# Seven block products for eight in the second expert's first matrix product

## The chip, the core and the metric

One core of one Trainium2 chip runs the whole program in one launch. The metric is the device time in microseconds; 753.59 us is the median of three runs of the kernel before. TensorE (PE) multiplies, VectorE (DVE), ScalarE (ACT) and GpSimd (POOL) do the rest, SyncE (SP) issues nearly all DMAs.

## The reference

Inputs: q, k, v of 2 batches x 8 heads x 768 positions x 64; a projection of 64 x 6; two experts' weights `w_in` (512 x 2048) and `w_out` (2048 x 512). q, k, v and the projection are float32; the four weight matrices are float64.

```python
def _attn_ref(q, k, v, proj):
    q_bucket, k_bucket = ...            # six sign bits of q @ proj and k @ proj
    mask = q_bucket[:, :, :, None] == k_bucket[:, :, None, :]
    scores = np.where(mask, (1 / np.sqrt(D)) * np.matmul(q, k.transpose(0, 1, 3, 2)), -1e9)
    attn = softmax(scores)
    return np.matmul(attn, v)

def _moe_ref(x, w_in, w_out):           # first expert, 1536 tokens
    h = x @ w_in
    return (h * (1 / (1 + np.exp(-h)))) @ w_out

def _moe2_ref(x, w_in, w_out):          # second expert, on the first one's output
    h = x @ w_in
    return (h - np.tanh(h)) @ w_out
```

Attention's output, transposed to 1536 tokens x 512, goes through the first expert and its output through the second.

## The kernel before

Every product of the experts is done to nearly float32's precision out of pairs: an operand is kept as a high part (rounded to the matrix unit's fp32r format) and a low part (the rest), and each product of two 128-deep blocks is three matmuls, high x high, high x low, low x high, added up in one PSUM bank. Names end in `h` and `l` for the two parts (`xh`/`xl`, `gh`/`gl`, a weight set's `wh`/`wl`).

Tokens lie on the free axis in four blocks of 384 (`NB`); blocks 0 and 1 are batch 0, blocks 2 and 3 batch 1; two of them are a pair. The model dimension (512) is four tiles of 128 (`KD`), the hidden dimension (2048) four chunks (`NCH`) of four tiles of 128 (`F`). For each chunk and pair the loops of lines 876 to 963 run: first product (`h_mm`, L892: for each block and each `f` 4 x 3 = 12 matmuls of 128x128 by 128x384), then tanh (`h_tanh`, L896), the gate (`h_gate`, in place in PSUM, L902 for the first expert, L904 for the second), high part of g (`h_hi`, copied through the helper on L334), low part of g (`h_lo`, L910, PSUM minus high part), then the second product (`o_mm`, L954, also 12 matmuls for each block and output tile), whose bank is added to an accumulator in SBUF (`o_acc`, L961; the first chunk copies, L959).

`PASSES` (L696) sets three passes: first expert on pair 0 (while batch 1's attention still runs), first expert on pair 1, second expert on both pairs. After the first expert's last chunk its sums are halved and split into the second expert's `xh`/`xl` (L968, L971).

Weights arrive as 64-bit floats in pieces of 128 x 512 (`load_w`, L785); five steps make float32 of them: absolute value on ScalarE (L817), clip on GpSimd or VectorE (L820), shift, sign, low word on VectorE (L823, L827, L831); then the high part on ScalarE (L835) and the low part on GpSimd or VectorE (L839). In the first pass the float32 pieces are also stored to DRAM and fetched again in the second. Chunks 1 and 3 of the later passes have a second set of weight tiles (`ww2`).

The order of all instructions on all engines is worked out when the program is built: each piece of work is a task (`add`) with engines and costs, a due time (`key`), dependencies, and buffers that it takes; `Plan.order` (L92) repeatedly gives an engine the task that can start first, with ties within `slack` broken by due time. Constants of the plan stand in `KNOBS`. What results is a fixed order per engine; at run time each engine goes through its own list and waits on semaphores. After attention there are six PSUM banks for products (`banks`) and two for the conversion of weights (`cvs`).

Of the kernel before, what the change touches and what calls it, by code (L numbers as in the profile page):

```python
# [21 lines left out]
W_MIN = 2.0 ** -15  # L22
W_MAX = 2.0 ** 16 * (1.875 - 2.0 ** -23)

KNOBS = dict(start=1.134, step=2.53, gap=9.343, step1=3.92, ffn=3.61, ffn3=2.222, pv=12.257, prep=16.11, hash=8.464,
             slack=0.042, conv=33.419, conv0=52.708, vld=10.124, vmax=13.049, vsplit=16.427, x2=0.271, direct=0.4,
             direct1=0.083, b_qh=1.32, b_qlo=100, b_kup=100, b_vlo=2, b_bi=2.75, b_thi=100, b_shi=0.98, b_slo=100,
             b_xh=1.72, b_xlo=1.56, b_wlo=100, b_clip=-0.24, b_hhi=0.67, k_m=-0.273, k_e=0.107, k_t=1.899,
             k_th=2.064, k_tl=2.019, k_hi=1.332, k_lo=1.98, k_f=3.209, cj=3.559, cl=7.897, ahead=2, by=3.547,
             xsets=0, raws=5, vmax1=70.287, emode=1, lmode=1)  # L30


class Slot:
# [166 lines left out]
def lsh_attention_moe_kernel(  # L200
# [12 lines left out]
    nc = tc.nc  # L213
# [96 lines left out]
    wr_slots = [Slot(), Slot()]  # L310
    for i, s in enumerate(wr_slots):
        s.tag = f"w{i}"
    wt_slots = slots(wt, "wa", 2, [128, 512], I32, "wa")
    th_slots = slots(gt, "th", 2, [128, NB], F32, "th")

    def get(h):
# [386 lines left out]

    def switch_two():
        es.close()
        for i in range(3):
            late[f"ps_n{i}"] = ctx.enter_context(tc.tile_pool(name=f"ps_n{i}", bufs=1, space=PSUM))
        for i in range(2):
            late[f"ps_d{i}"] = ctx.enter_context(tc.tile_pool(name=f"ps_d{i}", bufs=1, space=PSUM))
        late["ww2"] = ctx.enter_context(tc.tile_pool(name="ww2", bufs=1))  # L710
        late["acc2"] = ctx.enter_context(tc.tile_pool(name="acc2p", bufs=1))
        xp2 = ctx.enter_context(tc.tile_pool(name="xp2", bufs=1))
        for blk in (2, 3):
            xh.append(xp2.tile([128, KD, NB], F32R, name=f"xh{blk}"))
            xl.append(xp2.tile([128, KD, NB], F32R, name=f"xl{blk}"))

    second = add("", 0.0, switch_two, 0, last_attn + [first], takes=shut2)
    for x in shut2:
        x.users += 1
    second.opens = (*m_late, *cv_late)  # L720

    xready = {0: list(xdone[0]), 1: list(xdone[1])}
    t_two = t_ffn + 128 * K["ffn"]
    for blk in (2, 3):
        xready[blk] = []
        for dt in range(KD):
            def x_hi2(blk=blk, dt=dt):
                nc.scalar.copy(xh[blk][:, dt, :], x32[:, dt, (blk % 2) * NB:(blk % 2 + 1) * NB])

            def x_lo2(e, blk=blk, dt=dt):  # L730
                src = x32[:, dt, (blk % 2) * NB:(blk % 2 + 1) * NB]
                ENG[e].tensor_tensor(xl[blk][:, dt, :], src, xh[blk][:, dt, :].bitcast(F32), op=ALU.subtract)
            y = add("ACT", 0.52, x_hi2, t_two + K["x2"] + 0.1 * dt + blk, [second])
            xready[blk] += [y, add(("POOL", "DVE"), (1.02, 0.57), x_lo2, t_two + K["x2"] + 0.1 * dt + blk, [y], port=("DVE",), give="xlo")]

    seq = [0]
    wslots = [(wtile["h0"], wtile["l0"]), (wtile["h1"], wtile["l1"])]
    w2slots = [(Slot(),), (Slot(),)]
    acc2_slots = [Slot(), Slot()]
    stored = {}  # L740
    pieces = [0]

    def t_group(k):
        return t_ffn + K["ffn"] * k if k < 128 else t_two + K["ffn3"] * (k - 128)

    for ps_i, (e, fresh, blks) in enumerate(PASSES):
        pairs = [blks[i:i + 2] for i in range(0, len(blks), 2)]
        accs = {}
        xnext = {}
        for c in range(NCH):  # L750
            base = seq[0]
            two = ps_i > 0 and c % 2 == 1
            wset = []
            for m in range(2):
                held = Held(w2slots[m] if two else wslots[m])

                def w_tiles(m=m, held=held, two=two):
                    if held.tile is None:
                        shape = [128, KD, FW] if m == 0 else [128, F, DM]
                        pool = late["ww2"] if two else ww  # L760
                        held.tile = tuple(pool.tile(shape, F32R, tag=f"{x}{m}", name="w" + x) for x in ("h", "l"))
# [4 lines left out]
                for j in range(4):  # L766
# [20 lines left out]
                    ld = add("SP", 0.35, load_w, kj - K["cl"], [second] * two + ([stored[ps_i - 1, c, m, j]] if not fresh else []),  # L787
                             takes=[w], tail=1.65 if fresh else 0.82)
                    prior = [first_take] if first_take else [ld]
                    if not fresh:  # L790
# [74 lines left out]
            for pi, pair in enumerate(pairs):  # L865
# [62 lines left out]
                for q, blk in enumerate(pair):  # L928
# [4 lines left out]
                    for d in range(KD):  # L933
                        tk = t_group(seq[0])
                        seq[0] += 1
                        bk = Held(*banks)
                        fresh_acc = c == 0 and pr not in accs
                        if fresh_acc:
                            accs[pr] = Held((acc_slot,) if e == 0 else (acc2_slots[pr],))
                        ah = accs[pr]  # L940

                        def acc_tile(ah=ah, e=e, pr=pr, d=d, half=half):
                            if ah.tile is None:
                                pool = accp if e == 0 else late["acc2"]
                                ah.tile = pool.tile([128, KD, S], F32, tag="acc" if e == 0 else f"acc{pr}", name="acc")
# [18 lines left out]
                        ac = add("DVE", 0.55, o_acc, tk + 1, [om] + ([second] if e else []),  # L964
                                 takes=[ah] if fresh_acc else [], uses=[bk] + ([] if fresh_acc else [ah]))
                        if c == NCH - 1 and e == 0:
                            def y_hi(blk=blk, d=d, acc_tile=acc_tile):
                                nc.scalar.activation(out=xh[blk][:, d, :], in_=acc_tile(), func=ACTF.Copy, scale=0.5)  # L968

                            def y_lo(e, blk=blk, d=d, acc_tile=acc_tile):  # L970
                                ENG[e].scalar_tensor_tensor(xl[blk][:, d, :], acc_tile(), 0.5,  # L971
                                                               xh[blk][:, d, :].bitcast(F32), op0=ALU.mult, op1=ALU.subtract)
                            x = add("ACT", 0.525, y_hi, tk + 1.5, [ac], uses=[ah])
                            y = add("DVE", 0.56, lambda y_lo=y_lo: y_lo("DVE"), tk + 2, [x], uses=[ah], port=True)
                            xnext.setdefault(blk, []).extend([x, y])
                        elif c == NCH - 1:
                            add("SP", 0.35, lambda blk=blk, d=d, f=acc_tile: nc.sync.dma_start(
                                out=outT[d * 128:(d + 1) * 128, blk * NB:(blk + 1) * NB], in_=f()), tk + 2, [ac],
                                uses=[ah], tail=0.6)
        xready.update(xnext)  # L980

    for t in plan.order(K["slack"]):
        plan.run(t)
# [53 lines left out]
```

## Time and profile before

| | us |
|---|---|
| runs: lowest, median, highest of 3 | 753.16, 753.59, 754.58 |
| profiled execution | 754.19 |
| its span, first to last instruction | 752.3 |
| TensorE busy | 718.0 |
| VectorE, ScalarE, GpSimd busy | 531.6, 430.0, 370.3 |

The span is one execution of the program as the hardware profiler saw it. An engine's busy time is the union of its instructions; for TensorE the ends of overlapping matmuls are modelled. A time that ended an engine's idle stretch is put down to the engine that released it.

### The profile page before, as it was taken

To read this page: it belongs to the slowest core of one execution; us is meant where nothing else is said; L and a number is where in the kernel's file an instruction comes from. 1 tells how busy PE (TensorE), PEld (TensorE's weight loads), DVE (VectorE), ACT (ScalarE), POOL (GpSimd) and SP (SyncE) were. 2 spreads that over 40 slices of the span, in tenths; PEclk is the share of its full clock that TensorE was granted. 3 is DMA by queue.
4 is the path that set the end of the run, shared out by engine and by line. 5 is a ranking of instruction groups with operands and counts; after the bars stand their busy time and mean duration, and the time that the engine had idled before them with its cause. 6 is when DMAs were issued, how large, how long until landed. Compare 5 with 4: busy or idle time off the path is not lost.

```text
span 752.3 us, 14254 instructions
## 1 busy us (share of the span) xinstructions
PE 718.0 (95%) x5486; PEld 694.4 (92%) x5486; DVE 531.6 (71%) x1002; ACT 430.0 (57%) x813; POOL 370.3 (49%) x247
## 2 busy tenths in 40 slices
PE   5679889899999999999999999999999999999998
PEld 4478777799999999999999999999999999999998
DVE  6789899998897898977433689884685576344342
ACT  5879999996895966866442526542451434122130
POOL 5658779678798865677453353540341152000000
PEclk9799999999999999999999999999999999999999
DMA  9698999979899995982333333330131030000102
GB/s 358 138 219 164 182 194 240 246 151 257 240 236 244 215 228 152 236 183 71 103 102 96 104 121 112 113 112 30 56 113 56 1 103 10 1 1 1 63 22 85
DMA packets 140446, 100.78 MB, mean 134 GB/s; under 512 B 117438, under 2 KB 119742, under 8 KB 140378
## 3 DMA queue, kind: packets, MB, share of 16 engines
q1 hardware_dynamic: 140090, 99.59, 53.3%
q8 instruction: 43, 0.70, 0.4%
q10 hardware_dynamic: 288, 0.28, 0.2%
q14 instruction: 25, 0.20, 0.1%
HBM read 57.95 MB, written 11.53 MB: 92 GB/s over the span
## 4 chain that ended last, share of the span: by engine, by line
PE 66%; DVE 1%; ACT 0%; issue 0%; ACTq 0%; DVEq 0%
PE psm L954 32%; PE psm L892 30%; PE ps L554 2%; PE pso L631 1%; PE pso L632 1%; PE pso L633 1%; DVE p L558 0%; PE psm L414 0%; PE psm L665 0%; DVE wa L820 0%; DVE wa L831 0%; DVE acc L961 0%; ACT p L568 0%; DVE p L595 0%; DVE cv L827 0%
## 5 line engine op out<-in xcount | busy, mean ns | idle before, releaser
L892 PE MATMUL psm<-xh,wh 128*128 128x384 f32 x512 | 173.2, 338 | 0.7 <-ACT xh L334 0.4
L892 PE MATMUL psm<-xl,wh 128*128 128x384 f32 x512 | 172.4, 337 | 0.2 <-DVE xl L673 0.2
L892 PE MATMUL psm<-xh,wl 128*128 128x384 f32 x512 | 172.4, 337 | 0.0
L954 PE MATMUL psm<-gh,wh 128*128 128x384 f32 x512 | 172.3, 336 | 0.0
L954 PE MATMUL psm<-gh,wl 128*128 128x384 f32 x512 | 171.2, 334 | 0.0
L954 PE MATMUL psm<-gl,wh 128*128 128x384 f32 x512 | 171.2, 334 | 0.0
L613 POOL TENSOR_TENSOR hl<-p,hl 128x768 f16<-128x768 f32 x73 | 121.7, 1669 | 53.4 <-ACT hl L334 46.6
L839 POOL TENSOR_TENSOR wl<-wa,wh 128x512 fp32r<-128x512 f32 x64 | 83.2, 1302 | 107.9 <-ACT wh L835 107.5
L896 ACT ACTIVATE th<-psm 128x384 f32<-128x384 f32 x128 | 62.9, 492 | 102.8 <-PE psm L892 102.7
L558 DVE TENSOR_SCALAR_CACHE_REDUCE p<-ps 128x768 f32<-128x768 f32 x96 | 90.2, 951 | 14.7 <-PE ps L554 8.3
L910 DVE TENSOR_TENSOR gl<-psm,gh 128x384 fp32r<-128x384 f32 x128 | 70.7, 555 | 38.4 <-ACT gh L334 38.1
L961 DVE TENSOR_TENSOR acc<-acc,psm 128x384 f32<-128x384 f32 x96 | 52.8, 550 | 63.5 <-PE psm L954 63.4
L892 PEld LDWEIGHTS psm<-xh,wh 128*128 128x128 f32 x512 | 96.1, 188 | 1.5 <-DVE p L595 0.9
L892 PEld LDWEIGHTS psm<-xl,wh 128*128 128x128 f32 x512 | 96.2, 188 | 0.4 <-DVE xl L673 0.4
L954 PEld LDWEIGHTS psm<-gl,wh 128*128 128x128 f32 x512 | 96.2, 188 | 0.0
L892 PEld LDWEIGHTS psm<-xh,wl 128*128 128x128 f32 x512 | 96.1, 188 | 0.0
L954 PEld LDWEIGHTS psm<-gh,wh 128*128 128x128 f32 x512 | 96.1, 188 | 0.0
L954 PEld LDWEIGHTS psm<-gh,wl 128*128 128x128 f32 x512 | 96.1, 188 | 0.0
L554 PE MATMUL ps<-k,q 128*128 128x384 f32 x384 | 90.2, 362 | 5.0 <-DVE p L558 4.0
L568 ACT ACTIVATE p<-p,bi 128x768 f32<-128x768 f32 x96 | 89.3, 937 | 1.8
L334 ACT CAST gh<-psm 128x384 fp32r<-128x384 f32 x124 | 59.4, 481 | 50.5 <-DVE psm L904 36.2
L820 POOL TENSOR_SCALAR wa<-wa 128x512 f32<-128x512 f32 x33 | 63.7, 1931 | 43.9 <-ACT wa L817 43.7
(87 smaller groups left out, 1256.1 us busy)
## 6 DMA issues: line engine op xcount, KB each, us to landing
w<-in_w_in_dram SPq DMA_DIRECT2D x32, 512.0 KB
w<-in_w_out_dram SPq DMA_DIRECT2D x32, 512.0 KB
r<-in_qkT_dram SPq DMA_DIRECT2D x15, 768.0 KB
wi<-wa SPq DMA_DIRECT2D x16, 256.0 KB
wo<-wa SPq DMA_DIRECT2D x16, 256.0 KB
w<-wi SPq DMA_DIRECT2D x16, 256.0 KB
w<-wo SPq DMA_DIRECT2D x16, 256.0 KB
vr<-in_v_dram SPq DMA_DIRECT2D x6, 512.0 KB
```

The lines of the kernel that those rows point to most:

```text
L334: nc.scalar.copy(out, in_) if e == "ACT" else ENG[e].tensor_copy(out, in_)
L554: nc.tensor.matmul(out=get(ps)[:, u, 0:HS], lhsT=x[:, t * 128:(t + 1) * 128], rhs=c[:, u * HS:(u + 1) * HS], start=(j == 0), stop=(j == 1))
L558: nc.vector.tensor_scalar(get_p().rearrange("p (c s) -> p c s", c=2), get(ps)[:, :, 0:HS], FLOOR, None, op0=ALU.max, op1=ALU.max, accum_ou ...
L568: nc.scalar.activation(out=get_p(), in_=get_p(), func=ACTF.Exp, scale=0.125, bias=get(bi))
L613: ENG[e].tensor_tensor(get_hl()[:, 1, :], get_p(), get_hl()[:, 0, :], op=ALU.subtract)
L820: ENG[e].tensor_scalar(lead(), lead(), W_MIN, W_MAX, op0=ALU.max, op1=ALU.min)
L839: ENG[e].tensor_tensor(ll, get(wa).bitcast(F32), hh.bitcast(F32), op=ALU.subtract)
L892: nc.tensor.matmul(out=ps, lhsT=a[:, k, fs], rhs=b_[blk][:, k, :], start=(k == 0 and j == 0), stop=(k == KD - 1 and j == 2))
L896: nc.scalar.activation(out=get(th), in_=get(bk)[:, 0:NB], func=ACTF.Tanh, scale=0.5 if e == 0 else 1.0)
L910: nc.vector.tensor_tensor(g_tile(gl, "gl")[:, f, :], get(bk)[:, 0:NB], g_tile(gh, "gh")[:, f, :].bitcast(F32), op=ALU.subtract)
L954: nc.tensor.matmul(out=ps, lhsT=a[:, f, ds], rhs=b_.tile[:, f, :], start=(f == 0 and j == 0), stop=(f == F - 1 and j == 2))
L961: nc.vector.tensor_tensor(acc_tile(), acc_tile(), get(bk)[:, 0:NB], op=ALU.add)
```

## The change

The second expert leaves the general loop (`PASSES` keeps the first expert's two passes) and gets a loop of its own. Its first product uses Strassen's scheme in Winograd's form: in each chunk the 512 x 512 piece of `w_in` is taken as blocks by halves of the depth and by even and odd column tiles, the tokens of a pair as halves of the depth by the two blocks, and out of block sums made in fp32 seven products are formed, each 2 x 3 = 6 matmuls of 128x384 output, where eight such products gave the same four output tiles. A quad (`p`) is the seven products of two column tiles for one pair; a chunk has two pairs and two quads in each.

- The tokens: once per pair four block differences and seven splits into high and low part, instructions of 128 x 768, in place in the first expert's accumulator (`minus`, `split`), which is no longer halved; the factor one half is in the gate.
- The weights: per chunk four block sums in the two 128 x 1024 float32 tiles (`s_sum`, in place) and seven splits into one tile set `wsp` of seven operands (`s_split`). The second matrix is converted as before, into one of the two old sets.
- The quad: products 1, 6, 7, 5 open four banks; ScalarE copies two of them to SBUF, VectorE and GpSimd add; products 2, 4, 3 accumulate onto three of those banks after they have been read.
- The gate now reads PSUM and writes to SBUF; high and low part of g are made from that SBUF tile.
- Of the second product's first two groups the half on the older two g tiles is a task of its own (`half=2`).
- Seven banks for products and one for conversion after attention; `ww2` goes; in the second pass weights use the two sets and, for the first three chunks, the `wsp` tile.

```diff
-    PASSES = ((0, True, (0, 1)), (0, False, (2, 3)), (1, True, (0, 1, 2, 3)))
+    PASSES = ((0, True, (0, 1)), (0, False, (2, 3)))
...
-    m_late = [bank_slot(lambda i=i: late[f"ps_n{i}"]) for i in range(3)]
-    cv_late = [Slot(lambda i=i: late[f"ps_d{i}"].tile([128, 512], F32, tag="cv", name="cv")) for i in range(2)]
+    m_late = [bank_slot(lambda i=i: late[f"ps_n{i}"]) for i in range(4)]
+    cv_late = [Slot(lambda i=i: late[f"ps_d{i}"].tile([128, 512], F32, tag="cv", name="cv")) for i in range(1)]
...
-                held = Held(w2slots[m] if two else wslots[m])
+                if ps_i == 0:
+                    held = Held(wslots[m])
+                else:
+                    held = Held(*wslots, *([(ws_slot,)] if c < K["plain"] else []))
...
+        fin.append(split(0, 0, 0, here(0, 0) + [second]))
+        fin.append(split(1, 1, 0, here(1, 0) + [second]))
+        d_t1 = minus((0, 0), (0, 1), (0, 0), fin[0] + here(0, 1))
+        fin.append(split(2, 1, 1, here(1, 1) + [second]))
+        d_t3 = minus((0, 1), (1, 1), (0, 1), [d_t1] + here(1, 1))
+        d_t2 = minus((1, 1), (1, 1), (0, 0), fin[2] + [d_t1, d_t3])
+        fin.append(split(5, 1, 1, [d_t2]))
+        fin.append(split(6, 0, 1, [d_t3]))
+        fin.append(split(4, 0, 0, [d_t1, d_t2]))
+        d_t4 = minus((1, 0), (1, 0), (1, 1), fin[1] + [d_t2])
+        fin.append(split(3, 1, 0, [d_t4]))
...
+        a11 = s_split(0, 0, 0, got[0], ks)
+        a22 = s_split(3, 1, 1, got[1], ks + 0.5)
+        s1 = s_sum((1, 1), (0, 1), (1, 1), ALU.add, a22 + got[0], ks + 1)
+        s3 = s_sum((0, 1), (0, 0), (0, 1), ALU.subtract, [s1], ks + 1.5)
+        s2 = s_sum((0, 0), (1, 1), (0, 0), ALU.subtract, a11 + [s1, s3], ks + 1.6)
...
+                def product(o, bk, first, key, deps, pr=pr, p=p, s_tiles=s_tiles, sh=sh):
+                    def f():
+                        ps = get(bk)[:, 0:NB]
+                        sw, xw = s_tiles(), xops[pr](o)
+                        for k in range(2):
+                            for j, (a, b_) in enumerate(((0, 0), (0, 1), (1, 0))):
+                                nc.tensor.matmul(out=ps, lhsT=sw[a][:, o, 2 * k + p, :], rhs=xw[b_][:, k, :],
+                                                 start=(first and k == 0 and j == 0), stop=(k == 1 and j == 2),
+                                                 skip_group_check=True)
+                    return add("PE", 1.04, f, t_group(key), sdone[o] + xdone2[pr][o] + deps, takes=[bk] if first else [],
+                               uses=[sh] + ([] if first else [bk]), line="quad" if first else None)
...
+                p1 = product(0, al, True, kq, [])
...
+                c1 = hold(u2, al, t_group(kq + 0.5), p1)
+                p6 = product(5, be, True, kq + 0.5, [])
...
+                d2 = add("DVE", 0.55, lambda be=be, u2=u2: plus("DVE", get(u2), get(be)[:, 0:NB], get(u2)),
+                         t_group(kq + 1), [p6, c1], uses=[be, u2])
+                p7 = product(6, de, True, kq + 1, [])
+                c7 = hold(u3, de, t_group(kq + 1.5), p7)
+                p5 = product(4, ga, True, kq + 1.5, [])
+                d3 = add(("POOL", "DVE"), (1.02, 0.57), lambda e, u2=u2, u3=u3: plus(e, get(u3), get(u2), get(u3)),
+                         t_group(kq + 2), [d2, c7], uses=[u2, u3], port=("DVE",), give="u3")
+                p2 = product(1, al, False, kq + 2, [c1])
+                p4 = product(3, de, False, kq + 2.5, [c7])
+                d22 = add("DVE", 0.55, lambda be=be, ga=ga, u3=u3: plus("DVE", get(be)[:, 0:NB], get(ga)[:, 0:NB], get(u3)),
+                          t_group(kq + 2.6), [p5, d3], uses=[be, ga, u3])
+                p3 = product(2, ga, False, kq + 3, [d22])
+                d21 = add("DVE", 0.55, lambda de=de, u2=u2: plus("DVE", get(de)[:, 0:NB], get(de)[:, 0:NB], get(u2)),
+                          t_group(kq + 3), [p4, d2], uses=[de, u2])
+                d12 = add("DVE", 0.55, lambda ga=ga, u2=u2: plus("DVE", get(ga)[:, 0:NB], get(ga)[:, 0:NB], get(u2)),
+                          t_group(kq + 3.5), [p3, d2], uses=[ga, u2])
...
+                    def h_gate(bk=bk, th=th):
+                        nc.vector.scalar_tensor_tensor(get(th), get(bk)[:, 0:NB], 0.5, get(th), op0=ALU.mult,
+                                                       op1=ALU.subtract)
...
+                    def h_lo(e, f=f, th=th, gh=gh, gl=gl):
+                        ENG[e].tensor_tensor(g_tile2(gl, "gl")[:, f, :], get(th), g_tile2(gh, "gh")[:, f, :].bitcast(F32),
+                                             op=ALU.subtract)
...
+                    if q == 0 and d < K["half"]:
+                        om = add("PE", 1.04, lambda f=o_mm: f(range(2)), t_group(u0 + 6.6 + 0.1 * d),
+                                 wdone + [t for f in range(2) for t in gd[q, f]], takes=[bk], uses=[held, gh, gl])
+                        om = add("PE", 1.04, lambda f=o_mm: f(range(2, F)), tk, [om] + [t for f in (2, 3) for t in gd[q, f]],
+                                 uses=[bk, held, gh, gl])
```

In the quad `d3` may go to GpSimd only (`b_u3=100`), the low parts of weights too (`b_wl2=100`), the high parts of the split weights to ScalarE only (`b_sh=100`); clips and block sums prefer GpSimd, the low part of g prefers VectorE. `split`, `minus` and `s_split` name the blocks by (half of the depth, half of the columns or tokens).

## Rows read from the trace of the kernel before

**Rows 1.** The page's first part: busy us, share, instructions of each engine.
```profile
span 752.3 us, 14254 instructions
PE 718.0 (95%) x5486; PEld 694.4 (92%) x5486; DVE 531.6 (71%) x1002; ACT 430.0 (57%) x813; POOL 370.3 (49%) x247
```
**Rows 2.** Chain of waits, second expert: start us, us, what, number of instructions.
```profile
481.50 16.96 PE psm L892 x96
498.46 16.64 PE psm L954 x96
515.11 16.64 PE psm L892 x96
...
749.09 0.56 DVE acc L961
```
**Rows 3.** Busy us by stretch, second pass, then four chunks: engines, PEclk, DMA, GB/s.
```profile
348.38:481.50 133.12, 133.12 (x770) 133.12 (x769) 83.42 (x148) 63.71 (x126) 63.47 (x47) 1.00 0.35 103
481.50:548.39 66.89, 66.89 (x386) 66.89 (x385) 46.17 (x82) 25.90 (x52) 19.76 (x14) 1.00 0.23 72
548.39:615.27 66.88, 66.88 (x385) 66.88 (x385) 43.05 (x76) 24.08 (x49) 18.06 (x13) 1.00 0.20 63
615.27:682.16 66.89, 66.89 (x386) 66.89 (x385) 32.10 (x58) 18.22 (x38) 7.52 (x6) 1.00 0.05 16
682.16:749.09 66.93, 66.89 (x384) 66.57 (x383) 26.68 (x49) 15.57 (x32) 0.00 (x0) 1.00 0.12 45
```
**Rows 4.** The same view of two stretches beside attention.
```profile
160.00:180.00 20.00, 20.00 (x241) 19.08 (x238) 18.67 (x37) 18.32 (x32) 18.60 (x13) 1.00 0.98 234
...
130.00:140.00 10.00, 8.23 (x118) 7.13 (x117) 8.12 (x16) 8.23 (x15) 5.36 (x4) 0.92 1.11 287
```
**Rows 5.** Groups by line and shape, whole trace: busy us, mean ns, idle before.
```profile
L392 POOL TENSOR_TENSOR k<-r,k 128x768 fp32r<-128x768 f32 x15 | 27.6, 1840 | 0.8 <-ACT k L380 0.5
...
L732 POOL TENSOR_TENSOR xl<-x,xh 128x384 fp32r<-128x384 f32 x6 | 6.8, 1175 | 0.3 <-ACT xh L728 0.3
...
L334 ACT COPY x<-psm 128x384 f32<-128x384 f32 x8 | 3.4, 481 | 0.9 <-PE psm L665 0.8
...
L385 DVE TENSOR_TENSOR q<-r,q 128x768 fp32r<-128x768 f32 x1 | 1.0, 957 | 0.0
```
**Rows 6.** The same view of 481.5 to 749 us.
```profile
L904 DVE TENSOR_TENSOR psm<-psm,th 128x384 f32<-128x384 f32 x64 | 36.0, 563 | 27.6 <-ACT th L896 27.6
...
L827 DVE SCALAR_TENSOR_TENSOR cv<-w,cv 128x512 int32<-128x512 int32 x20 | 13.8, 690 | 0.3
L823 DVE TENSOR_SCALAR cv<-wa 128x512 int32<-128x512 int32 x20 | 13.7, 687 | 4.3 <-POOL wa L820 4.3
L831 DVE SCALAR_TENSOR_TENSOR wa<-w,cv 128x512 int32<-128x512 int32 x20 | 13.6, 681 | 0.2
...
L820 DVE TENSOR_SCALAR wa<-wa 128x512 f32<-128x512 f32 x10 | 7.0, 702 | 5.7 <-ACT wa L817 5.5
...
L839 POOL TENSOR_TENSOR wl<-wa,wh 128x512 fp32r<-128x512 f32 x21 | 27.1, 1294 | 81.7 <-ACT wh L835 81.6
L820 POOL TENSOR_SCALAR wa<-wa 128x512 f32<-128x512 f32 x10 | 19.2, 1919 | 22.8 <-ACT wa L817 22.8
```
**Rows 7.** Two lines' instructions: duration ns min/median/max, first and last start us.
```profile
L910 DVE TENSOR_TENSOR gl<-psm,gh x128: 518/558/560, 149.1 to 734.1; 128x384 fp32r<-128x384 f32 x128
...
L971 DVE SCALAR_TENSOR_TENSOR xl<-acc,xh x16: 545/578/1656, 333.2 to 484.4; 128x384 fp32r<-128x384 f32 x16
```
**Rows 8.** Timeline, last chunk's last first-product group: start us, us, engine, what.
```profile
732.25 0.33 PE L954 MATMUL psm<-gh,wh 128*128 128x384 f32 x1
...
732.50 0.49 ACT L896 ACTIVATE th<-psm 128x384 f32<-128x384 f32 x1 [0.47 <-PE psm L892]
...
734.14 0.56 DVE L910 TENSOR_TENSOR gl<-psm,gh 128x384 fp32r<-128x384 f32 x1 [0.55 <-ACT gh L334]
```

More of the change, by code (lines that the diff above doesn't have):

```diff
@@ L312, in lsh_attention_moe_kernel @@
         s.tag = f"w{i}"
-    wt_slots = slots(wt, "wa", 2, [128, 512], I32, "wa")
+    wa_pair = wt.tile([128, 2, 512], I32, name="wa")
+    wt_slots = [Slot(lambda i=i: wa_pair[:, i, :]) for i in range(2)]
     th_slots = slots(gt, "th", 2, [128, NB], F32, "th")
@@ L705, in switch_two @@
         es.close()
-        for i in range(3):
+        for i in range(4):
             late[f"ps_n{i}"] = ctx.enter_context(tc.tile_pool(name=f"ps_n{i}", bufs=1, space=PSUM))
-        for i in range(2):
-            late[f"ps_d{i}"] = ctx.enter_context(tc.tile_pool(name=f"ps_d{i}", bufs=1, space=PSUM))
-        late["ww2"] = ctx.enter_context(tc.tile_pool(name="ww2", bufs=1))
+        late["ps_d0"] = ctx.enter_context(tc.tile_pool(name="ps_d0", bufs=1, space=PSUM))
+        late["wsp"] = ctx.enter_context(tc.tile_pool(name="wsp", bufs=1))
         late["acc2"] = ctx.enter_context(tc.tile_pool(name="acc2p", bufs=1))
@@ L715, in switch_two @@
             xl.append(xp2.tile([128, KD, NB], F32R, name=f"xl{blk}"))
+        for pr in range(2):
+            late["xt", pr] = tuple(xp2.tile([128, 3, 2, NB], F32R, name=f"{x}{pr}") for x in ("xth", "xtl"))
     second = add("", 0.0, switch_two, 0, last_attn + [first], takes=shut2)
@@ L719, in lsh_attention_moe_kernel @@
         x.users += 1
[L720 removed]
     xready = {0: list(xdone[0]), 1: list(xdone[1])}
[L723 removed]
+    t_one = t_ffn + 16 * NCH * K["ffn"]
+    t_two = t_one + 16 * NCH * K["ffn2"]
     for blk in (2, 3):
@@ L785, in load_w @@
                         nc.sync.dma_start(out=w.rearrange("p n t -> p (n t)") if fresh else w, in_=src)
-                    ld = add("SP", 0.35, load_w, kj - K["cl"], [second] * two + ([stored[ps_i - 1, c, m, j]] if not fresh else []),
+                    ld = add("SP", 0.35, load_w, kj - K["cl"], ([] if fresh else [stored[ps_i - 1, c, m, j]]),
                              takes=[w], tail=1.65 if fresh else 0.82)
@@ L963, in lsh_attention_moe_kernel @@
                         om = add("PE", 2.08, o_mm, tk, wdone + gdone[q], takes=[bk], uses=[held, gh, gl])
-                        ac = add("DVE", 0.55, o_acc, tk + 1, [om] + ([second] if e else []),
+                        ac = add("DVE", 0.55, o_acc, tk + 1, [om] + ([second] if ps_i else []),
                                  takes=[ah] if fresh_acc else [], uses=[bk] + ([] if fresh_acc else [ah]))
[L966 to L979, printed above, removed]
@@ L980, in lsh_attention_moe_kernel, with operand, src, here @@
-        xready.update(xnext)
+                        if c == NCH - 1:
+                            ydone[blk, d] = ac
+        for pr, ah in accs.items():
+            yheld[pr] = (ah, tk)
+    xops, xdone2 = {}, {}
+    for pr in range(2):
+        ah, tk = yheld[pr]
+        ah.users += 1
+        ka, kb = 2 * pr, 2 * pr + 1
+        xth, xtl = (None, None)
+        def operand(i, pr=pr, ka=ka, kb=kb):
+            if i in (3, 5, 6):
+                j = {5: 0, 6: 1, 3: 2}[i]
+                return tuple(x[:, j] for x in late["xt", pr])
+            blk, lo = {0: (ka, 0), 1: (ka, 2), 2: (kb, 2), 4: (kb, 0)}[i]
+            return xh[blk][:, lo:lo + 2, :], xl[blk][:, lo:lo + 2, :]
+        def src(kappa, nu, ah=ah):
+            return ah.tile[:, 2 * kappa:2 * kappa + 2, nu * NB:(nu + 1) * NB]
+        def here(kappa, nu, ka=ka, kb=kb):
+            return [ydone[(ka, kb)[nu], d] for d in (2 * kappa, 2 * kappa + 1)]
+        k0 = t_two + K["xprep1"] if pr else t_one + K["xprep"]
+        kd = K["xk1"] if pr else 4.0
+        count = [0]
+        def split(i, kappa, nu, deps, operand=operand, src=src, ah=ah, k0=k0, kd=kd, count=count):
+            def f_hi(e):
+                copy(e, operand(i)[0], src(kappa, nu))
+            def f_lo(e):
+                hi, lo = operand(i)
+                ENG[e].tensor_tensor(lo, src(kappa, nu), hi.bitcast(F32), op=ALU.subtract)
+            key = k0 + kd * count[0]
+            count[0] += 1
+            x = add(("ACT", "DVE"), (0.85, 0.6), f_hi, key, deps, uses=[ah], port=("DVE",), give="xph")
+            y = add(("POOL", "DVE"), (1.84, 0.95), f_lo, key + 0.1, [x], uses=[ah], port=("DVE",), give="xpl")
+            return [x, y]
+        def minus(out, p, q, deps, src=src, ah=ah, k0=k0, kd=kd, count=count):
+            def f(e):
+                ENG[e].tensor_tensor(src(*out), src(*p), src(*q), op=ALU.subtract)
+            return add(("POOL", "DVE"), (1.84, 0.95), f, k0 + kd * count[0] - 0.5 * kd, deps, uses=[ah], port=("DVE",),
+                       give="xpl")
+        fin = []
+        fin.append(split(0, 0, 0, here(0, 0) + [second]))
[9 more added lines that the diff above has]
+        fin.append(split(3, 1, 0, [d_t4]))
+        xops[pr] = operand
+        xdone2[pr] = {i: f for i, f in zip((0, 1, 2, 5, 6, 4, 3), fin)}
+        last_prep = [t for f in fin for t in f]
+        end = add("", 0.0, None, k0, last_prep)
+        for h in (ah,):
+            end.uses = end.uses + (h,)
@@ new lines, in lsh_attention_moe_kernel @@
+    spare = add("", 0.0, None, 0, [t for blk in (2, 3) for t in xready[blk]])
+    xflat = x32.rearrange("p k s -> p (k s)")
+    tmp_slots = [Slot(lambda i=i: xflat[:, i * NB:(i + 1) * NB]) for i in range(4)]
+    th_late = Slot(lambda: xflat[:, 4 * NB:5 * NB])
+    pair_late = Slot(lambda: xflat[:, 5 * NB:5 * NB + 1024].bitcast(I32).rearrange("p (a n) -> p a n", a=2))
+    for s in tmp_slots + [th_late, pair_late]:
+        s.open = False
+    spare.opens = (*tmp_slots, th_late, pair_late)
+    ths = one(th_slots + [th_late])
```

242 lines of the change are left out of this document (223 added, 19 removed).

## The prediction, made before the run

> **What bounds the kernel now.** I read the page's busy shares first, then the chain of waits, then busy time by stretch. TensorE is busy 95% of the span [rows 1], which proves little, because its matmuls overlap; the chain of waits settles it. From 340 us on that chain is nothing but TensorE: one stage of 96 matmuls behind the other, 16.64 us each, with no other engine's piece between, up to the last accumulation at 749.09 us [rows 2]. The second expert is the last 16 of these stages: four chunks of the hidden dimension, in each of them first product (L892) and second product (L954) for two pairs of token blocks. Its span by stretch is four chunks of 66.9 us [rows 3], all of it TensorE time at a granted clock of 1.00, the 2.4 GHz level. So in this part a matmul that goes away is worth its pitch, as long as nothing else becomes late. The pitch is 16.64/96 = 0.1733 us; in the first L892 stage of each chunk it is 16.96/96 = 0.1767 us [rows 2].
>
> **What goes away.** The first product of the second expert is 8 stages x 96 = 768 matmuls, 4 x 16.96 + 4 x 16.64 = 134.4 us. Seven block products of six matmuls replace eight, so 672 stay: 134.4/8 = 16.8 us less. That is the whole gain that I can find; the second product, the first expert, attention, the weights' transfers and the final stores keep their counts. A chunk becomes 66.9 - 4.2 = 62.7 us.
>
> **What is added beside it, per chunk** (four quads; a quad is the seven products that give two 128-wide column tiles of the hidden dimension for the two token blocks of a pair):
> - ScalarE: two copies out of PSUM per quad, 8 x 0.481 [rows 5] = 3.8 us. It was busy 25.9 of 66.9 us in the fullest chunk [rows 3]: hidden.
> - VectorE: four sums per quad with one PSUM operand; the nearest row is L904, 0.563 [rows 6]. 16 x 0.563 = 9.0 us.
> - GpSimd: one sum per quad, 4 x 1.175 [rows 5] = 4.7 us.
> - Weights: the input matrix is split into high and low part 7 times in place of 4 (three more low parts at 1.294 on GpSimd [rows 6], 3.9 us), after four block sums (on GpSimd about 1.3, as L839 has the same elements; on VectorE about 0.7, as the 512-wide rows have).
> - Gate and low part of g count as before, but the low part is now a subtraction of two SBUF tiles.
> - Once: the block sums and splits of the tokens, 11 two-operand instructions of 128x768 per pair, 0.957 on VectorE [rows 5] or 1.840 on GpSimd [rows 5]. Pair 0's lie in the first expert's second pass, 133 us in which VectorE is busy 83 and GpSimd 63 [rows 3]: nothing. Pair 1's can start only when that pass ends and are wanted one half chunk, 31 us, later: 10.5 us on VectorE or 20.2 on GpSimd. The 16 conversions that they replace go.
>
> Loads then. The last chunk has no weight conversion: VectorE 26.7 us [rows 3] + 9.0 = 35.7 of 62.7 us. A chunk that converts the next one's eight weight pieces adds 8 x (0.687 + 0.690 + 0.681) = 16.5 us [rows 6], and 0.7 a piece when the clip comes to VectorE too: 52 to 58 of 62.7, 83 to 92%, where the fullest chunk now has 46.2 of 66.9. GpSimd stands at 8 clips x 1.919 + 11 low parts x 1.294 + 4.7 = 34 us, 55%. Nothing is over its capacity, so TensorE stays the bound on average. Such loads alone don't stop it: from 160 to 180 us VectorE and GpSimd are both 93% busy and TensorE has no gap [rows 4].
>
> **What can come late.** Now the groups of 12 matmuls (12 x 0.1733 = 2.08 us) are independent of each other, and TensorE reads g a whole stage after its first group. In a quad it waits for other engines twice, and both waits have little slack.
> (a) The last product accumulates onto the bank of the fourth and may start only after a VectorE sum has read that bank, and this sum needs the GpSimd sum, which needs a ScalarE copy of the third product. From the quad's start: third product out at 3.12, 0.25 to the next engine [rows 8], copy 0.48, sum 1.18, sum 0.56, three hand-overs of about 0.05: 5.75 us, against six products of 1.04 = 6.24. Slack 0.5 us. A clip in front on GpSimd takes 1.919, a conversion step on VectorE 0.69.
> (b) After the second quad, second product's groups need the g of the sixth product. Now tanh, gate, high and low part take from 732.50 to 734.14 + 0.56, 2.2 us, after 0.25 us [rows 8]; with the extra sum in front 0.25 + 0.56 + 0.05 + 2.2 = 3.06. TensorE has the seventh product (1.04) and two half groups on the older g (2.08) to do: 3.12. Slack nil. In the first half of a chunk the next pair's products can be put in front; in the second they can't, as the tile of the split weights has one copy and is refilled only after the chunk's last product.
> (c) The refill: 7 high, 7 low parts and 4 sums. The low parts take 9.1 us of GpSimd; with the two or three sums that a later split waits for, some 12 us, under 8 second-product groups, 16.64 us, and the last block is wanted 6 us later still. Nothing, with 4 us or more of cover.
>
> No row shows such a wait under this load, so I bound the sum of (a) and (b). At best nothing: the slacks hold. At worst each of the 16 quads loses one clip, 16 x 1.919 = 31 us. A gain below nothing is excluded, as the chain here holds no time of another engine to win. My value: in the 12 quads of the three converting chunks 0.3 us each (one conversion step of 0.69 met in about half of them), 3.6 us; for (b) 0.4 us in three chunk ends, 1.2 us; nothing in the last chunk. 4.8 us, nearer the best end, because the row of 160 to 180 us is the one of like load and has no gap.
>
> The first 340 us only see new due times (gap, conv, conv0 move by under 0.7 us) and a seventh bank in place of a second conversion bank after the switch. The order may shuffle: I take 0, and 1.5 us either way for the range.
>
> **Sum.** On the profiled execution: 754.19 us, of which 752.3 is the span and 1.9 lies around it [rows 1]. 754.19 - 16.8 + 4.8 = 742.2 us; the median shown is 0.6 us under the profiled one: 741.6 us.
>
> **The row on the low part of g.** The low part read from PSUM took 518 to 560 ns in 128 instructions, with no exception; L971, the same width with both inputs in SBUF, took 545 to 1656 [rows 7]. The change turns the first kind into the second for 64 instructions, 8 of which close chain (b). The Trainium skill says why this would be so (SBUF — State Buffer, Who interferes with whom): a VectorE instruction with two SBUF inputs shares a read port with GpSimd, and whichever comes second waits for the whole of the other. By that rule the long cases are GpSimd's instructions seen from VectorE, and the trace agrees (1656 is near 545 plus a low part). If the low part kept its 0.56 the sum above stands, 741.6; by the rule it is rival 2's 748, whose price is worked out from rows 7 alone.
>
> **Rivals.**
> 1. No stall: the slacks hold as the order intends. 754.19 - 16.8 - 0.6 = 736.8 us. For it: 267 us without a gap now; against: slack nil in (b). With the shuffle of the first part 736 to 739. Chance 0.23.
> 2. The port: the g chain's last step meets a GpSimd instruction in the 6 half chunks that convert (6 x 1.1 = 6.6 us more, 1656 - 545), beside the 4.8. 748 us, 746 to 752. For it rows 7; against: the half groups of (b) could be refilled by the next pair's products in three of the six. Chance 0.17.
> 3. VectorE with GpSimd becomes the bound: in-order queues at 83 to 92% put a clip or two conversion steps into every quad's chain (a). The place is the wait of the seventh product. The break-even is 16.8/16 = 1.05 us a quad; at 1.919 in each quad it is 736.8 + 30.7 = 767.5 us, at 1.4 759. For it: in 130 to 140 us VectorE at 81% and TensorE only 82% busy, its clock at 0.92 [rows 4]; against: four of 16 quads run without conversion, and the pieces' due times leave an order in which sums go first. Chance 0.13; and 0.06 for landing within 0.2% of before.
> 4. It doesn't do what it says: the product isn't the shorter, because the pitch rises to the slower one, 0.1767, in all 672. Then 672 x 0.1767 = 118.7 against 117.6, 1 us: inside the forecast's range.
>
> **From these to the numbers.** Forecast, 739 to 746: 0.41. With rival 1 (0.23) and rival 2 (0.17) faster makes 0.81; same 0.06; slower 0.13; 0.2%, 1.5 us, is what a measurement of this kernel can tell from no change. The range reaches from rival 1's 736.8 less a little, 736.5, to 753, just beyond rival 2: outside it lie rival 3, half of "same" and a shuffle to the good, 0.2 together.
>
> **What would show it.** Right: first-product stages of 14.6 us in the chain of waits, second-product stages of 16.64 us as before, and idle time of TensorE in the second expert of some 5 us, released by VectorE's sums (a) and by the low part of g (b), and less of it in the last chunk. Rival 1: chain of TensorE alone again. Rival 2: low parts of g with a maximum well above 0.6 us and TensorE waiting for them. Rival 3: the chain runs through VectorE and GpSimd, over 1 us idle per quad. Wrong altogether: TensorE waiting for the refill, for pair 1's tokens, or a first part (up to 340 us) that moved by more than 1.5 us.

## Result, and the profile after

The changed kernel takes 745.42 us (median of four runs, 744.35 to 746.36) beside 753.89 us for the kernel before: ratio 0.9887, 95% interval 0.9869 to 0.9906, 8.5 us less. The forecast was 741.6 us and 12 less. The profiled execution is the longest of the four, 746.36 us.

The page's first part, after. The columns are those of [rows 1].
```profile
span 744.6 us, 14192 instructions
PE 704.2 (95%) x5390; PEld 679.6 (91%) x5390; DVE 558.3 (75%) x1025; ACT 452.2 (61%) x853; POOL 504.3 (68%) x340
```
TensorE has 96 matmuls fewer. GpSimd took on most of the new work, 134 us of it.

Busy time by stretch, as in [rows 3], near the second expert's first, third and fourth chunk.
```profile
483.50:546.60 63.10, 59.79 (x332) 58.58 (x331) 51.73 (x83) 32.22 (x62) 54.42 (x37) 0.97 0.23 72
...
608.80:671.60 62.80, 61.87 (x356) 61.55 (x355) 48.23 (x82) 29.21 (x58) 43.91 (x33) 1.00 0.17 51
671.60:744.60 73.00, 69.46 (x399) 68.82 (x397) 35.03 (x63) 20.04 (x42) 15.84 (x15) 0.99 0.12 44
```
VectorE's load is at or under the estimate: 48 to 52 us in a chunk that converts (52 to 58 forecast), 35 in the last. GpSimd's is above it: 44 to 54 us (34 forecast). It took over 29 of the 64 low parts of g at about 1.02 us and makes three block sums of 1.29 us a chunk, which the forecast named and did not add in; in the first chunk pair 1's tokens come on top. TensorE has gaps in the first and the third chunk. The granted clock is 0.97 in the first.

The second expert lasted 749.07 - 481.50 = 267.6 us before and 741.11 - 483.43 = 257.7 us now, from the end of the first expert's last matmul to the end of its own: 9.9 us less. The end of the chain of waits, after:
```profile
726.96 14.15 PE psm L1321 x80
...
741.14 0.56 DVE acc L1328
```
TensorE's lost time in the second expert (starts of consecutive matmuls more than 0.3 us apart, less the pitch of 0.1733, summed; also used below) was nothing before and is 6.5 us now. It is lost at three places, but for 0.2 us. The first is the start. The chain of waits from 483 us on, after: start us, us, what.
```profile
483.71 2.60 POOL wa L1093
...
486.33 0.70 DVE cv L1096
...
487.06 0.69 DVE cv L1101
487.76 0.47 DVE acc L975
...
488.25 0.83 ACT xh L338
489.08 0.38 ACT x L1239
...
490.15 0.83 ACT xth L338
490.99 0.39 ACT x L1239
...
491.42 3.69 PE psm L1229 x12
```
Read from below: TensorE waits for ScalarE's copy of a product (L1239). In ScalarE's fixed order a token split of pair 1 (L338, `xh`) stands in front of it. That split waits for the first expert's last accumulation (L975), which stands in VectorE's queue behind two conversion steps (L1096, L1101), and these wait for a GpSimd clip (L1093) that took 2.60 us, where the others take 1.92; it began at 483.71, beside a token difference on VectorE (L1026, 482.60 to 484.52). So one clip holds up, through three queues, a copy that has nothing to do with it. The second wait is of the same kind: the next copy stands behind the split `xth`, which waits for a token difference on GpSimd (L1026). TensorE's timeline of the same place, start us and us:
```profile
487.30 0.34 PE L1229 MATMUL psm<-xh,wl 128*128 128x384 f32 x1
489.51 0.44 PE L1229 MATMUL psm<-xh,wh 128*128 128x384 f32 x1 [1.87 <-ACT x L1239]
...
491.42 0.69 PE L1229 MATMUL psm<-xth,wh 128*128 128x384 f32 x1 [0.60 <-ACT x L1239]
...
492.23 0.52 PE L1229 MATMUL psm<-xth,wl 128*128 128x384 f32 x1
492.55 0.52 PE L1229 MATMUL psm<-xth,wh 128*128 128x384 f32 x1
```
Two waits cost 2.0 and 0.8 us beyond the pitch. After the second, nine matmuls start 0.32 us apart in place of 0.173, 1.4 us more. The granted clock there is 0.52, the 1.2 GHz level; columns as in [rows 3]:
```profile
491.90:494.42 2.52, 2.52 (x10) 2.52 (x9) 2.52 (x2) 2.06 (x4) 2.52 (x3) 0.52 0.00 0
```

The other two places are chain (a). The chain of waits before the matmul at 533.49, and before the one at 652.91:
```profile
528.74 1.92 POOL x L1093
...
530.85 1.02 POOL gl L1279
531.87 0.97 POOL x L1245
...
532.87 0.58 DVE psm L1245
...
533.49 1.32 PE psm L1229 x6
```
```profile
649.02 1.93 POOL x L1093
...
650.97 0.71 DVE cv L1096
...
652.30 0.57 DVE psm L1245
...
652.91 2.20 PE psm L1229 x11
```
At 533 a clip and a low part of g stand on GpSimd in front of the quad's sum; at 652 a clip holds VectorE's conversion steps, which stand in front of the quad's last sum. 1.0 and 1.1 us. Chain (b) has 0.2 us at one place.

Outside the second expert, TensorE's own stage (48 matmuls of L954, L968 now) begins at 341.99 us, 1.9 later than the 340.06 of before. Chain of waits, before and after:
```profile
340.06 8.32 PE psm L954 x48
```
```profile
341.99 8.32 PE psm L968 x48
```

### The profile page after: what moved, and what is told of

Its sections match the earlier page's. It is cut to its first block, busy times and chain, and to the rows that moved or that the text cites. A ratio compares the mean times of both kernels' runs of the same rounds, so it can differ in the third digit from the quotient of the medians.

```text
span 744.6 us, 14192 instructions
## 1 busy us (share of the span) xinstructions
PE 704.2 (95%) x5390; PEld 679.6 (91%) x5390; DVE 558.3 (75%) x1025; ACT 452.2 (61%) x853; POOL 504.3 (68%) x340
## 4 chain that ended last, share of the span: by engine, by line
PE 65%; ACT 9%; DVE 7%; POOL 7%; DMA 7%; issue 4%; SPq 0%; POOLq 0%; ACTq 0%; DVEq 0%
PE psm L1321 14%; PE psm L1229 13%; PE psm L906 13%; PE psm L968 11%; PE ps L558 6%; ACT p L572 2%; DMA w<-in_w_in_dram 2%; PE psm L418 2%; POOL wl L810 2%; POOL x L1093 2%; PE pso L635 2%; PE pso L636 1%; PE pso L637 1%; ACT hl L338 1%; DMA w<-in_w_out_dram 1%
## 5 line engine op out<-in xcount | busy, mean ns | idle before, releaser
L906 PE MATMUL psm<-xh,wh 128*128 128x384 f32 x256 | 86.9, 340 | 1.1 <-DVE p L599 0.7
L968 PE MATMUL psm<-gh,wh 128*128 128x384 f32 x256 | 86.7, 339 | 0.0
L906 PE MATMUL psm<-xl,wh 128*128 128x384 f32 x256 | 86.2, 337 | 0.2 <-DVE xl L677 0.2
L906 PE MATMUL psm<-xh,wl 128*128 128x384 f32 x256 | 86.1, 336 | 0.0
L968 PE MATMUL psm<-gh,wl 128*128 128x384 f32 x256 | 85.7, 335 | 0.0
L968 PE MATMUL psm<-gl,wh 128*128 128x384 f32 x256 | 85.7, 335 | 0.0
L558 PEld LDWEIGHTS ps<-k,q 128*128 128x128 f32 x384 | 67.4, 197 | 8.8 <-DVE p L562 4.6
L810 POOL TENSOR_TENSOR wl<-w,wh 128x512 fp32r<-128x512 f32 x32 | 44.6, 1403 | 37.1 <-ACT wh L806 37.0
L338 ACT CAST hl<-p 128x768 f16<-128x768 f32 x71 | 59.1, 833 | 0.5
L635 PEld LDWEIGHTS <-pt 128*128 128x128 f16 x438 | 40.0, 97 | 15.0 <-DMA pt<-hl 8.1
L635 PE MATMUL pso<-v,pt 128*128 128x65 f16 x438 | 47.8, 195 | 6.2 <-DMA pt<-hl 6.0
L853 POOL TENSOR_TENSOR wl<-wa,wh 128x512 fp32r<-128x512 f32 x32 | 42.1, 1317 | 12.2 <-ACT wh L849 11.9
L906 PEld LDWEIGHTS psm<-xh,wh 128*128 128x128 f32 x256 | 48.1, 188 | 1.9 <-DVE p L599 1.2
```

The source lines that it names most:

```text
L338: nc.scalar.copy(out, in_) if e == "ACT" else ENG[e].tensor_copy(out, in_)
L558: nc.tensor.matmul(out=get(ps)[:, u, 0:HS], lhsT=x[:, t * 128:(t + 1) * 128], rhs=c[:, u * HS:(u + 1) * HS], start=(j == 0), stop=(j == 1))
L635: nc.tensor.matmul(out=o, lhsT=pt[:, kt, :], rhs=v16[:, kt, h, :], start=(kt == 0), stop=False)
L810: ENG[e].tensor_tensor(ll, w_tile(), hh.bitcast(F32), op=ALU.subtract)
L853: ENG[e].tensor_tensor(ll, get(wa).bitcast(F32), hh.bitcast(F32), op=ALU.subtract)
L906: nc.tensor.matmul(out=ps, lhsT=a[:, k, fs], rhs=b_[blk][:, k, :], start=(k == 0 and j == 0), stop=(k == KD - 1 and j == 2))
```

## Experiments

TensorE's lost time is of the second expert, in the profiled execution.

**The changed kernel again.** No edit.

> The changed kernel itself, to stand beside the others on the same chip. In its trace TensorE reaches the first stage that it has to itself 1.9 us later than before, and loses 4.0 us (2.0 + 0.8 waiting, 1.2 at the lower clock) at the start of the second expert, 1.0 us at 533 and 1.1 us at 653. If these are the order of work, they stand in this run within 0.3 us each, and the time is 745.4 within 1. If they are scatter of single runs, at least one of them is gone or moved by over 1 us.

Measured: 744.15 us, ratio 0.9857 (0.9833 to 0.9881); lost 5.9 us: 1.5 + 0.8 and ten slow matmuls at the start, 1.0 at 533, 0.9 at 652. The same places, the first wait 0.5 us shorter (0.3 was allowed) and the others within 0.3: the lost time belongs to the order of work. The own stage begins at 342.91, another 0.9 us later than in the first profile.

**Copies first.**
```diff
+        late_prep = [fin[2][0], d_t3, d_t2, fin[3][0], fin[4][0], fin[5][0], d_t4, fin[6][0]]
...
                 c7 = hold(u3, de, t_group(kq + 1.5), p7)
+                if c == pr == p == 0:
+                    for t in late_prep:
+                        t.deps.append(c7)
```


> In the order of work, pair 1's token differences and splits that need the first expert's last sums are put behind ScalarE's two copies of the first quad. Theory A (ScalarE's queue: the copy stood behind a token split that waited for the last accumulation): the 4.0 us at the start of the second expert, lower clock included, fall under 1 us, and the time is 3 us under the changed kernel's, about 742.5. Rival B (VectorE and GpSimd are overloaded in the first half chunk, wherever the copies stand): pair 1's tokens come late and the time returns within the next 40 us, as waits for tokens or for VectorE's sums: the time stays within 1 us of the changed kernel's.

Measured: 747.03 us, 0.9892 (0.987 to 0.9915): slower than the changed kernel beside it by 2.9 us; lost 7.7 us. The first wait is gone and the slow matmuls with it. But 0.8 us are lost at 488, where a copy stands behind a weight's split, and 1.1 at 491, where the quad's sum stands behind a token difference on VectorE; 1.7 and 0.7 come at 504 and 507, 0.8 and 0.4 at 537, 0.8 at 590 and 1.0 at 654. Chain of waits before the first of the new ones, of this kernel:
```profile
500.21 0.72 ACT xh L338
...
503.06 2.18 DVE gl L1283
505.23 0.94 DVE psm L1246 x2
```
Theory A fails as a remedy: the token work that was moved back stands in the next quads' way, and a low part of g takes long on VectorE, 2.18 us. The waits within the next 40 us looked like rival B, load, though the time missed B's too (within 1 us); the short clip and the new order below show that load is not the cause.

**The eighth product back.**
```diff
-                        for k in range(2):
+                        for k in (0, 1, 0, 1) if o == 0 else (0, 1):
...
-                    return add("PE", 1.04, f, t_group(key), ...
+                    return add("PE", 2.08 if o == 0 else 1.04, f, t_group(key), ...
```


> Each quad's first product is done twice over (its second time starts the bank afresh), which puts back the 96 matmuls and changes nothing else of the scheme. Theory A (TensorE is the bound, and the gain is the count of matmuls): 96 x 0.175 = 16.8 us more than the changed kernel, less what the longer quad takes off its waits, at most 4 us: 758 to 762 us, which is 4 to 8 us above the kernel before. Rival B (VectorE with GpSimd is the bound of the second expert): under 8 us more, below 753.

Measured: 763.84 us, 1.0119 (1.0089 to 1.0149), 19.7 us above the changed kernel beside it; lost 8.0 us. So 16.8 us for the matmuls, some 2 us for longer waits, and the rest within the runs' scatter. B is out: TensorE is the bound and the gain is the count of its matmuls. It came out above A's upper end because the new order has two waits of 2.3 and 2.4 us. The first one's start is again a clip: L1093 from 589.87 to 591.80, then a conversion step, then the quad's sum, then the matmul at 593.77. The longer one has the same chain, from a clip at 659.42 to the matmul at 663.31, and ten slow matmuls behind it.

**The earlier due times.**
```diff
-    ..., gap=9.388, ..., conv=32.734, conv0=53.318, ..., cl=8.822, ...
+    ..., gap=9.343, ..., conv=33.419, conv0=52.708, ..., cl=7.897, ...
```


> The changed kernel with the earlier due times of the weights' conversion and of the second batch (gap, conv, conv0, cl as before). Theory A (these due times shift VectorE's order from 95 us on and cost the 1.9 us that the changed kernel is late at 340 us): TensorE's stage of its own begins at 340 in place of 342 us and the time is 1 to 2 us under the changed kernel's. Rival B (scatter of runs of the attention part): the start of that stage and the time stay within 0.7 us of the changed kernel's run beside it.

Measured: 742.9 us, 0.9844 (0.982 to 0.9868); own stage from 342.10, not 340, so the due times aren't what delays it: A is out there. B's 0.7 us was too narrow for both, as the start is 0.8 us earlier and the time 1.25 us less than the changed kernel's, with overlapping intervals, so a small gain is neither shown nor excluded; lost 4.1 us with the same waits (1.2 + 0.8, 1.2, 0.8) and no slow matmuls in this profile.

**The kernel before, twice more.**

> The kernel before, looked at again, for the start of the stage that TensorE has to itself. It stood at 340.1 us before the change and at 340.5 to 343.4 in nine profiles of the changed kernel and its variants, whose first part has the same TensorE order. Theory A (the change, by its banks or its conversion tiles, costs the first part 2 us): 339.5 to 340.6 again. Rival B (scatter from run to run): a start anywhere from 340 to 343.5 us.

> The kernel before once more, for the same question. Theory A: 339.5 to 340.6 us in both. Rival B: at least one of the two above 341.

Measured: 755.98 and 755.20 us, one run each. The own stage and the second expert's first stage in the chain of waits, of the one and of the other:
```profile
341.86 8.32 PE psm L954 x48
...
483.31 16.96 PE psm L892 x96
```
```profile
341.08 8.32 PE psm L954 x48
...
482.53 16.96 PE psm L892 x96
```
Rival B: the start moves from run to run in the kernel before too, and 340.06 was an early one. From there on that kernel takes the same time each run (141.4 us to the second expert in all three).

**The clip made short.**
```diff
-  ENG[e].tensor_scalar(val().bitcast(F32), val().bitcast(F32), W_MIN, W_MAX, ...)
+  ENG[e].tensor_scalar(val().bitcast(F32)[:, 0:16], val().bitcast(F32)[:, 0:16], W_MIN, W_MAX, ...)
```


> The order of work on every engine is the changed kernel's, instruction for instruction; only the clip in the second expert's weight conversion works on 16 of 512 columns (it leaves out the limits on the other weights' magnitude). So a clip lasts some 0.1 us in place of 1.92 on GpSimd and 0.7 on VectorE. Theory A (chain (a): the GpSimd sum, or the shift on VectorE, stands behind a clip): the waits near 533 and 653 us fall from 1.0 and 0.9 to under 0.2, the two at the start of the second expert from 1.5 to 2.0 and 0.8 to under 0.5 with no spell at the lower clock: TensorE's lost time goes from 6.3 to under 2 us, the time to 739 to 741. Rival B (VectorE's conversion steps of 0.69 and the token work are in front, not the clip): at least 4 us stay lost and the time is above 742.

Measured: 738.81 us, 0.9772 (0.9754 to 0.9791), lost 0.2 us. Half of the clips (the other half alike), of the changed kernel and of this one: duration ns min/median/max.
```profile
L1093 POOL TENSOR_SCALAR wa<-wa x16: 1910/1916/2639, 409.2 to 640.2; 128x512 f32<-128x512 f32 x16
```
```profile
L1093 POOL TENSOR_SCALAR wa<-wa x16: 252/262/269, 408.9 to 634.5; 128x16 f32<-128x16 f32 x16
```
With the order unchanged and the clip at 0.26 us (not the 0.1 expected), every wait of TensorE but chain (b)'s 0.2 us goes, those at the start too. All 32 clips are on GpSimd, and the order was planned with 1.29 us for each: 0.6 us too little. VectorE is as busy as before, 52 us in the first chunk. A holds (the time is just under its range), and the load of VectorE is not what costs time. GpSimd's load fell with the clips, from 54 to 45 us in the first chunk, so this run alone does not part its load from the clips' place.

**Chain (b) without its cover.**
```diff
-    ..., half=2, ...
+    ..., half=0, ...
```


> The split of the second product's first two groups is taken back (half=0): chain (b) keeps its 3.06 us, and its cover is the seventh product alone, 1.04. Theory A (chain (b) is as long as worked out, and the next pair's products can be put in front only within a chunk): about 2 us of waiting in front of the second product at each of the four ends of a chunk, released by the low part of g, little at the four half chunks: 8 us more than the changed kernel, 752 us. Rival B (chain (b) is shorter in fact, or VectorE does other things first either way): under 3 us more, below 747.5.

Measured: 755.33 us, 1.0009 (0.9992 to 1.0026), level with the kernel before; lost 15.0 us. The last chunk shows the chain as worked out. Chain of waits from the last product on, of this kernel:
```profile
730.28 0.50 ACT x L1269
...
730.80 0.56 DVE x L1272
...
731.82 0.47 DVE psm L1245
...
732.86 0.55 DVE gl L1279
733.42 0.48 DVE th L1272
...
733.92 0.52 ACT gh L338
...
734.47 0.57 DVE gl L1279
...
735.08 15.20 PE psm L1321 x86
```
Against the changed kernel it is 1.5% by the two ratios, 11 us where A said 8; the places are A's only in part. At the last end, the time from the sum to the low part, 732.86 to 735.04, is the 2.2 us worked out, second-product groups that were ready went first, and 1.25 us stayed. At the three inner ends the next chunk's first products had been put in front and waited for the refilled weights (0.9 + 0.9 us at the second and at the third). Around the first, from 530 to 543, these waits, a copy, a quad's sum and matmuls at the lower clock took 8.2 us.

**More cover for chain (b).**
```diff
-    ..., half=2, ...
+    ..., half=4, ...
```


> The split is widened to four groups (half=4), 2.08 us more cover for chain (b). Theory A (chain (b) costs only the 0.2 us that its one gap near 727 us shows): within 1 us of the changed kernel's 744 to 745.5, the waits of chain (a) where they were. Rival B (chain (b) is met in places where the matmuls only run late rather than stop): 2 us faster or more.

Measured: 744.96 us, 0.9855 (0.9839 to 0.9871), as the changed kernel again (0.9857); lost 6.4 us, at the start, at 526, 530 and 541. A: (b) was covered already, and its one wait of 0.2 us is gone. But chain (a)'s waits did not stay where they were, as A had said: the one at 652 is gone, a copy is late at 526, and at 541 TensorE waits for the refilled weights:
```profile
542.17 0.45 PE L1229 MATMUL psm<-xh,wl 128*128 128x384 f32 x1 [0.51 <-POOL wl L1181]
```

**The order planned anew.**
```diff
-            a = add(("POOL", "DVE"), (1.29, 0.42), c_clip, ...
-            a = add("DVE", 0.6, c_shift, ...
+            a = add(("POOL", "DVE"), (1.92, 0.69), c_clip, ...
+            a = add("DVE", 0.69, c_shift, ...
...
-    xprep=14.912, xprep1=2.896, xk1=2.806, convo=54.917, convh=37.499, fill=14.668, convo0=35.195, convh0=75.173,
-    fill0=45.82, ..., cj2=5.837, half=2, b_xph=1.92, b_xpl=-0.35, b_cl2=2.16, ..., b_ss=1.98, b_u3=100, b_hh2=1.76, b_hl2=-0.24
+    xprep=26.181, xprep1=16.387, xk1=4.874, convo=58.994, convh=29.792, fill=16.815, convo0=23.339, convh0=100.867,
+    fill0=62.405, ..., cj2=5.42, half=4, b_xph=1, b_xpl=-0.3, b_cl2=0.166, ..., b_ss=0, b_u3=2, b_hh2=0, b_hl2=-1.087
```
(ffn3=2.266 too, and gap, conv, conv0 and cl as in the experiment with the earlier due times.)

> The order is planned anew: the clip at its measured 1.92 (GpSimd) and 0.69 (VectorE) and the shift at 0.69 in place of 1.29, 0.42 and 0.6, due times and preferences of the second expert's weight and token work moved, half=4, the first part's due times as before the change. Theory A (the lost time is a matter of where a clip or a token split stands in the fixed order, not of load): TensorE's lost time in the second expert falls under 2 us, and the time to 738 to 741. Rival B (load: VectorE at 80 to 85% and GpSimd at 70 to 87% must hold up a chain with 0.5 us of slack somewhere): 4 us or more stay lost, in other places, and the time is above 742.5.

Measured: 737.87 us, 0.9767 (0.9746 to 0.9788): the fastest, with every computation of the changed kernel in place. Lost nothing. Busy time by stretch and the end of the chain of waits:
```profile
483.50:546.00 62.50, 62.50 (x362) 62.50 (x361) 51.75 (x89) 33.78 (x64) 47.22 (x34) 1.00 0.22 68
546.00:608.00 62.00, 62.00 (x358) 62.00 (x357) 50.29 (x86) 29.67 (x60) 40.03 (x31) 1.00 0.22 69
```
```profile
484.37 13.69 PE psm L1229 x78
...
718.31 16.66 PE psm L1321 x96
...
734.99 0.56 DVE acc L1328
```
VectorE is as loaded as in the changed kernel (51.7 of 62.5 us), GpSimd a little less (47), and the chain is TensorE's alone: 734.97 - 484.37 = 250.6 us, 17.0 less than before. GpSimd's 47 us lose nothing here, where 44 us in the changed kernel's third chunk lose 1.1 us: so it is the place and not the amount of the work that decides. Rival B is out. The plan changed in costs, due times and preferences together; which of them did it was not separated.

## Why the prediction came out as it did

- **What goes away, 16.8 us: right.** 17.0 us in the retimed kernel, where nothing else is in the way; at least 16.8 back when the eighth product returns. Rival 1's 736.8 us, no stall, is about what the kernel takes once the waits are gone: 738.81 us with the short clip, 737.87 retimed.
- **Loads below capacity: right.** TensorE stays the bound, and the same load of VectorE runs with no gap (retimed). GpSimd's came out 10 to 20 us a chunk above the 34 forecast.
- **What comes late, 4.8 us: the term that was mis-sized.** 6.5 us in the first profile, 5.9 in the second. Its two parts were placed wrongly. I spread chain (a) over 12 quads at 0.3 us; it came in two quads at 1 us, 2.1 us for the 3.6 forecast, each time from a clip on, the 1.9 us instruction I had named, and not from the 0.69 us step I counted with. Chain (b) was given 1.2 us and took 0.2. So the two terms took 2.3 of the 4.8 us, and the rest was lost where nothing had been forecast (next point): that the sums are near each other is luck.
- **Pair 1's tokens, no term in the sum: the step that failed.** I priced that work by VectorE's and GpSimd's capacity over 31 us; its high parts on ScalarE (0.83 us each) I did not price, the quad's copies there I called "hidden", and on VectorE an instruction of this work took up to 1.92 us where 0.957 was priced. Its place in ScalarE's queue, ahead of these copies, cost 2.8 us, and the spell at the lower clock that followed 1.4 us: 4.2 of the 6.5. TensorE waiting on account of pair 1's tokens is one of the signs that the prediction gave for "wrong altogether"; the count of matmuls held all the same (last chunk's first-product stage of 84 matmuls in 14.75 us, 14.6 forecast). Capacity says nothing on what an in-order engine waits for at the head of its queue. The short clip shows where that wait came from.
- **Refill: right** in the changed kernel (one wait of the weight load on L1181, 0.3 us, which moves no matmul). Its 4 us of cover depend on the order: TensorE waits for it with half=0, and 0.5 us with half=4.
- **Rival 2, the port:** the low part of g on VectorE took 548 to 1578 ns, against 518 to 560 before [rows 7]. The two lines of it on VectorE, after:
```profile
L1279 DVE TENSOR_TENSOR gl<-th,gh x22: 548/716/1578, 498.9 to 726.8; 128x384 fp32r<-128x384 f32 x22
...
L1279 DVE TENSOR_TENSOR gl<-x,gh x13: 549/953/1491, 496.1 to 724.7; 128x384 fp32r<-128x384 f32 x13
```
  The trace agrees with the Trainium skill (SBUF — State Buffer, Who interferes with whom) that two SBUF inputs make VectorE wait for GpSimd. All 24 that took over 0.6 us in this profile began while a GpSimd sum or subtraction of two SBUF tiles was running, and ended 0.41 to 0.42 us after its end. So the wait is for the rest of that instruction, and not for a whole one, as the prediction read the 1656 ns. TensorE's weight load waited for such a low part only once, 0.4 us, so the price of 6.6 us did not come; 29 of the 64 were on GpSimd.
- **First part, 0 with 1.5 either way:** scatter of 340.1 to 343.4 us over twelve profiles, the kernel before included (340.1, 341.1, 341.9); wider than I allowed. The means are 341.0 for three profiles of before and 342.2 for nine of the others: that the change has a share of 1 us is neither shown nor excluded. The 1.9 us of the first profile is over the 1.5 that the prediction named as a sign of being wrong, and the kernel before shows as much by itself.
- So 741.6 was 3.8 us too low against the first median and 2.6 against the second: 1.7 and 1.1 us by the lost time (6.5 and 5.9 for 4.8), the rest by the first part and within the runs' spread of 2 to 4 us.

## What to carry to other kernels

Where the order per engine is fixed at build time, one instruction of 1.9 us in front of a chain with 0.5 us of slack is paid for by the engine that bounds the kernel. That the plan put it there because its cost was 0.6 us short is likely and not shown: no run changes that cost alone. Still, measure the durations of helper work before tuning the due times (here 1.92 for the planned 1.29, and the kernel before had it in [rows 6]). Fewer matmuls were worth their full pitch once the order was right. Price moved work by who stands behind it in each queue, not by the engine's spare capacity.

## What the runs showed of the hardware

Short waits of TensorE can cost more than their length. In the changed kernel it stood idle for 1.87 and 0.60 us, with six matmuls between, and the next nine ran at the 1.2 GHz level (0.32 us apart); with 1.37 and 0.60 us in the run again, ten; with 1.00 and 0.59 us in the run with the earlier due times, none. In the run with the eighth product back ten followed a single wait of 2.22 us and none one of 2.11. A GpSimd clip of 128x16 still takes 0.26 us, and one of 128x512 takes 1.92, where its subtraction of two tiles of that size takes 1.29 to 1.30. The clip on VectorE, where the retimed order puts 14 of 32, takes 0.43 us as a rule and up to 1.09 (three of the 14 over 1 us).
